# Scores of the third chunk computed early in fp32 and parked in DRAM, and key blocks of nearly equal size, in a top-k attention followed by two MLPs

## The chip, the cores and the metric

The kernel runs on one core of one Trainium2 chip. The metric is the device time of one launch in microseconds (us); the median of three runs of the kernel before is 1254.39 us (1254.22 to 1255.24).

## What is computed

Four batches of eight heads, 576 positions, 64 numbers to a head. For every query row only the 32 largest of the 576 scores are kept, the softmax is taken over those, and the result of all heads goes, token by token, through two MLPs with 2304 tokens, a model width of 512 and a hidden width of 2048.

```python
scores = scale * np.matmul(q, k.transpose(0, 1, 3, 2))
kth = np.partition(scores, -top_k, axis=-1)[..., -top_k:-top_k + 1]
scores = np.where(scores >= kth, scores, -1000000000.0)
attn = np.exp(scores - np.max(scores, axis=-1, keepdims=True))
attn = attn / (np.sum(attn, axis=-1, keepdims=True) + 1e-09)
x = np.matmul(attn, v)            # to (B * S, H * D)
h = x @ w_in;  g = h - np.tanh(h);                                     x = g @ w_out
h = x @ w_in2; g = np.where(h > 0, h, np.exp(np.minimum(h, 0)) - 1);   out = g @ w_out2
```

## The kernel before

The 2304 tokens are cut into six chunks of 384 tokens (chunk 0 to chunk 5; "the third chunk" is chunk 2, all of batch 1, tokens 192 to 575). A chunk has four pairs of heads, and each pair has two groups of three query tiles (128 query rows by 576 scores each), so there are 48 groups, numbered `g.at` 0 to 47; groups 16 to 23 are chunk 2. In chunks 0, 2, 3 and 5 a unit (`Unit`) is one head of a pair, and so is a group; in chunks 1 and 4 a unit holds 192 rows of both heads.

For every tile `scores` (L286) makes the 128x576 scores in two halves of 288. Chunk 0 (`u.whole`) multiplies fp32 operands directly, one matmul call for a half (L297; the profile shows two rows for each fp32 call). All later chunks first split q and k into two fp32r parts (`split_qk` at L257: ScalarE copies, GpSimd subtracts; tiles `qs`, `kk`) and use two fp32r matmuls for a half (L299, L300). ScalarE copies each half from PSUM (tile `ps`) to the score tile `s` in SBUF (L301), of which there are seven.

The search (`topk_steps`, L303) runs on VectorE: four rounds, in each a MAX8 that finds the next eight maxima (L322), and after the first three a MATCH_REPLACE that takes them out (L336). Then the mask is applied: by VectorE (L343), or by ScalarE (L338, L339) for all tiles of most groups of chunk 0. `transposed` (L345) transposes the masked weights `e` in five blocks of keys with TensorE (L364) and copies them out as `ph` (L365); `attend` (L367) multiplies each block of keys of `ph` with the same block of v (`vraw`) (L386), both heads side by side in the columns of the array. The blocks are 128, 128, 128, 128 and 64 keys.

The MLPs follow a chunk behind: `first` (L458) is the first product of a step (twelve matmuls of 384 columns into `h`, L471), ScalarE evaluates the nonlinearity (`t`), `gate` (L480) combines both on VectorE (L485, L490), ScalarE and GpSimd split it into `gh` and `gl` (L130, L131), and `second` (L496) accumulates nine matmuls of 512 columns into `acc` (L507). Each chunk has 2 x 16 such steps; `between` (L513) turns the first MLP's output into the second's input (`zh`, `zl`). The weights are not stored as fp32r, so in the first stretch and during chunk 0's MLPs `prepare` (L154) unpacks them: load `wr`, ScalarE (L165, L166, L170), GpSimd (L168), VectorE (`wf`, L171), split (`wp`), and a store to a scratch in DRAM (L176), from where later chunks load them (`wt`, L187).

What stands where in the program is set by ticks: a group's search takes four ticks (round r of group n is tick 4n + r), and tables `before`, `mid`, `late`, `ends` name what else is issued at a tick. A list scheduler then orders the instructions of each engine by priority, which follows this order of issue; from there each engine takes its instructions in that fixed order. All DMAs of the program are issued by SyncE (SP), also in one fixed order, and a DMA whose wait isn't met holds up those behind it.

Of the kernel before, what the change touches and what calls it, by code (L numbers as in the profile page):

```python
# [8 lines left out]
F32 = mybir.dt.float32  # L9
# [88 lines left out]
def tile_topk_attention_two_mlps(  # L98
# [34 lines left out]
    def bank(tag, name, bufs):  # L133
        return ps.tile([P, 512], F32, tag=tag, name=name, bufs=bufs)
# [63 lines left out]
    for ci, size in enumerate(SIZES):  # L198
        for p in range(NPAIR):
            row = []  # L200
            c0 = 0
            for b, q0, n in CHUNKS[ci]:
                for heads in ([[0], [1]] if n >= 256 else [[0, 1]]):
                    u = Unit()
                    u.ci, u.b, u.p, u.q0, u.heads, u.c0, u.n = ci, b, p, q0, heads, c0, n
                    u.id = f"{ci}_{p}_{b}_{q0}_{heads[0]}"
                    u.whole = ci < WHOLE
                    u.last = False
                    u.k = n * len(heads) // P
                    row.append(u)  # L210
                c0 += n
# [27 lines left out]
    def quick(u):  # L239

        return u.ci < QUICK and u.p == NPAIR - 1 and u.g.at == chunk_end[u.ci] - 1

    def load_q(u):
        u.qraw = sb.tile([P, NU], F32, tag="qraw", name=f"qraw{u.id}", bufs=QR_BUFS)
        src = qT[u.b, 2 * u.p + u.heads[0] : 2 * u.p + u.heads[-1] + 1, :, u.q0 : u.q0 + u.n].rearrange("h d s -> d h s")
        nq = u.n * len(u.heads)
        for half in range(1 if u.whole else 2):
            nc.sync.dma_start(u.qraw[half * D : half * D + D, :nq].rearrange("d (h s) -> d h s", s=u.n), src)

    def load_k(u):  # L250
        u.kraw = {}
        for h in u.heads:
            u.kraw[h] = sb.tile([P, S], F32, tag="kraw", name=f"kraw{u.id}_{h}", bufs=KR_BUFS)
            for half in range(1 if u.whole else 2):
                nc.sync.dma_start(u.kraw[h][half * D : half * D + D], kT[u.b, 2 * u.p + h])

    def split_qk(u):  # L257

        if u.whole:
            return  # L260
        u.kh, u.kl = {}, {}
        nq = u.n * len(u.heads)
# [14 lines left out]
    def segments(u, t):  # L277
# [5 lines left out]
                out.append((lo, hi, h, t * P + lo - i * u.n))  # L283
        return out

    def scores(u, t):  # L286
        if t == 0:
            u.s = []
        s = sb.tile([P, S], F32, tag="s", name=f"s{u.id}_{t}", bufs=S_BUFS)
        u.s.append(s)  # L290
        for half in range(2):
            cs = slice(half * HS, half * HS + HS)
            for lo, hi, h, _ in segments(u, t):
                pt = bank("at", f"ps{u.id}_{t}_{half}_{h}", 3)
# [395 lines left out]
```

## Time and profile before

| | us |
|---|---|
| median of three runs | 1254.39 |
| the profiled execution | 1255.49 |
| its span, first to last instruction | 1253.7 |
| TensorE (PE) busy | 1173.3 |
| VectorE (DVE) busy | 981.0 |
| ScalarE (ACT) busy | 783.6 |
| GpSimd (POOL) busy | 605.1 |

The profiled execution took 1.8 us more than its span, and 1.1 us more than the median. TensorE's busy time counts overlapping matmuls once, and a busy TensorE may still be at half clock. The mean granted clock over the span is 0.969 of 2.4 GHz.

### The profile page before, as it was taken

What the parts mean: (1) busy time and instruction counts of PE and PEld (TensorE: products, weight loads), DVE (VectorE), ACT (ScalarE), POOL (GpSimd) and SP (SyncE); (2) the same over time, 40 slices, a digit from 0 to 9 for tenths busy, and PEclk for the clock granted to TensorE, in tenths of its full rate; (3) what the DMA queues carried; (4) which work ended last, traced back from release to release, by engine and by line L of the source; (5) the groups of instructions that cost most, each with busy time, mean ns of one, the idle gap of its engine ahead of it and who ended that gap; (6) DMA issues with size and microseconds to landing.
All of it is one profiled execution on the core that took longest, in us unless ns stands there. A gap on an engine that the chain in (4) does not pass through costs nothing.

```text
span 1253.7 us, 19743 instructions
## 1 busy us (share of the span) xinstructions
PE 1173.3 (94%) x6424; PEld 982.7 (78%) x6424; DVE 981.0 (78%) x1951; ACT 783.6 (63%) x1716; POOL 605.1 (48%) x629
## 2 busy tenths in 40 slices
PE   4477889999999999999999999999999999999998
PEld 2243468877879888988888989888888888889897
DVE  7899999999999999959989768899779998100111
ACT  5898878789776557545566565666555565332333
POOL 4787459978994433333433344434334422223222
PEclk9975689998999999999999999999999999999999
DMA  7987247986779775667656778667667545687672
GB/s 238 319 285 251 84 155 233 354 274 222 265 245 358 238 227 168 226 223 262 213 195 204 236 229 271 217 190 239 210 225 259 198 153 179 208 273 254 219 248 79
DMA packets 97446, 286.12 MB, mean 228 GB/s; under 512 B 12096, under 2 KB 27968, under 8 KB 97344
## 3 DMA queue, kind: packets, MB, share of 16 engines
q1 hardware_dynamic: 97344, 284.87, 68.5%
q8 instruction: 51, 0.84, 0.3%
q14 instruction: 51, 0.42, 0.1%
HBM read 246.55 MB, written 38.27 MB: 227 GB/s over the span
## 4 chain that ended last, share of the span: by engine, by line
PE 70%; ACT 8%; DVE 8%; DMA 6%; POOL 5%; issue 3%; SPq 0%; ACTq 0%; POOLq 0%; DVEq 0%
PE acc L507 28%; PE h L471 28%; PE av L386 6%; DMA wr<-in_w_dram 5%; PE pt L364 4%; DVE vm L322 3%; DVE w L336 2%; PE ps L299 2%; PE ps L300 2%; POOL wr L168 2%; DVE wf L171 1%; ACT s L301 1%; ACT wr L166 1%; POOL kk L131 1%; ACT ph L365 1%
## 5 line engine op out<-in xcount | busy, mean ns | idle before, releaser
L131 POOL TENSOR_TENSOR gl<-g,gh 128x384 fp32r<-128x384 f32 x192 | 205.1, 1070 | 356.8 <-ACT gh L130 322.4
L322 DVE MAX8 vm<-w 128x8 f32<-128x576 f32 x432 | 317.9, 750 | 3.3
L507 PE MATMUL acc<-wt,gh 128*128 128x512 f32 x1008 | 269.0, 397 | 0.4 <-ACT gh L130 0.3
L336 DVE MATCH_REPLACE8 w<-vm,w 128x576 f32<-128x576 f32 x288 | 213.0, 740 | 0.0
L507 PEld LDWEIGHTS acc<-wt,gh 128*128 128x128 f32 x1008 | 184.7, 188 | 34.6 <-issue 3.9
L364 PE MATMUL pt<-ident,e 128*128 128x128 f32 (+1 forms) x720 | 120.1, 297 | 46.7 <-ACT e L339 35.5
L130 ACT ACTIVATE gh<-g 128x384 fp32r<-128x384 f32 x192 | 100.5, 524 | 80.0 <-DVE g L485 45.4
L301 ACT ACTIVATE s<-ps 128x288 f32<-128x288 f32 (+1 forms) x320 | 122.1, 407 | 43.6 <-PE ps L300 36.1
L485 DVE SCALAR_TENSOR_TENSOR g<-t,h 128x384 f32<-128x384 f32 x96 | 52.0, 543 | 123.8 <-ACT t L477 123.8
L507 PE MATMUL acc<-wt,gl 128*128 128x512 f32 x504 | 148.8, 398 | 0.0
L471 PE MATMUL h<-zh,wt 128*128 128x384 f32 (+2 forms) x768 | 146.7, 325 | 1.6 <-ACT zh L526 0.9
L364 PEld LDWEIGHTS pt<-ident,e 128*128 128x128 f32 (+1 forms) x720 | 89.8, 145 | 71.5 <-ACT e L339 42.2
L322 DVE MAX8 vm<-s 128x8 f32<-128x576 f32 x144 | 108.0, 750 | 47.1 <-ACT s L301 46.6
L471 PE MATMUL h<-xh,wt 128*128 128x384 f32 x672 | 141.9, 338 | 0.0
L471 PEld LDWEIGHTS h<-zh,wt 128*128 128x128 f32 x768 | 124.9, 189 | 9.1 <-ACT zh L526 2.4
L365 ACT ACTIVATE ph<-pt 128x384 f32<-128x384 f32 (+1 forms) x240 | 109.6, 491 | 25.3 <-PE pt L364 24.3
L471 PEld LDWEIGHTS h<-xh,wt 128*128 128x128 f32 x672 | 117.9, 188 | 7.1 <-issue 0.6
L343 DVE SCALAR_TENSOR_TENSOR e<-s,vm,e 128x576 f32<-128x576 f32 x115 | 116.3, 1017 | 1.6 <-ACT e L326 0.8
L476 ACT ACTIVATE t<-h 128x384 f32<-128x384 f32 x96 | 46.5, 486 | 102.6 <-PE h L471 102.5
L507 PEld LDWEIGHTS acc<-wt,gl 128*128 128x128 f32 x504 | 92.6, 188 | 18.3 <-issue 0.6
L336 DVE MATCH_REPLACE8 w<-vm,s 128x576 f32<-128x576 f32 x144 | 106.7, 741 | 0.0
L168 POOL TENSOR_TENSOR wr<-wr,tiny 128x512 f16<-128x512 f32 x64 | 90.1, 1410 | 31.8 <-ACT wr L166 28.5
(80 smaller groups left out, 2019.3 us busy)
## 6 DMA issues: line engine op xcount, KB each, us to landing
wt<-w SPq DMA_DIRECT2D x336, 512.0 KB, 4.3
wr<-in_w_dram SPq DMA_DIRECT2D x64, 512.0 KB, 5.3
w<-wp SPq DMA_DIRECT2D x64, 512.0 KB, 4.3
kraw<-in_kT_dram SPq DMA_DIRECT2D x120, 144.0 KB, 4.2
vraw<-in_vL_dram SPq DMA_DIRECT2D x64, 160.0 KB, 3.0
qraw<-in_qT_dram SPq DMA_DIRECT2D x88, 96.0 KB, 3.4
out_dram<-o SPq DMA_DIRECT2D x16, 256.0 KB, 5.4
out_dram<-o SPq DMA_DIRECT2D x4, 128.0 KB, 4.9
```

Of the source, the lines that this page charges most:

```text
L130: nc.scalar.activation(hi, src, copy)
L131: nc.gpsimd.tensor_sub(lo, src, f(hi))
L168: nc.gpsimd.tensor_mul(top, scaled, tiny)
L301: nc.scalar.activation(s[lo:hi, cs], pt[lo:hi, :HS], copy)
L322: nc.vector.max(g.vm[:, j, min(r, 1)], u.s[t] if r == 0 else g.w[j])
L336: nc.vector.match_replace(g.w[j], v, u.s[t] if r == 0 else g.w[j], FILL)
L343: nc.vector.scalar_tensor_tensor(u.e[t], u.s[t], v[:, 7:8], u.e[t], op0=ALU.is_ge, op1=ALU.mult, accum_out=g.sum[:, j : j + 1])
L364: nc.tensor.transpose(pt[:kn, j * P : j * P + P], v.e[t][:, k0 : k0 + kn], ident)
L365: nc.scalar.activation(g.ph[:kn, blk, :nq], pt[:kn, :nq], copy)
L386: nc.tensor.matmul(banks[c0][h * D : h * D + D, : v.n], v.vraw[h][:kn, blk], v.g.ph[:kn, blk, cs], start=(blk == order[0]), stop=(blk == o ...
L471: nc.tensor.matmul(h[:, cs], wv[:, wi, kt], xs[:, kt, cs], start=(a == 0), stop=(a == len(jobs) - 1))
L507: nc.tensor.matmul(acc[ci, m][t], gx[:, t * P : t * P + P], wt[:, wi], start=(ft == 0 and k == 0), stop=(ft == NF - 1 and k == 2),)
```

## The change

Two things change. First, the blocks of keys become 116, 116, 116, 116 and 112 (the host lays out v for them; a block is still stored and loaded with 128 rows). Second, the scores of groups 16 to 23 (`PARK`) are no longer made just ahead of their search. They are made while chunk 0 is searched, from tick 4 on, a unit every 3.5 ticks, at a priority lowered by 300 places (`later`): `park` multiplies in fp32 as chunk 0 does, into PSUM banks of the tag `h`, ScalarE copies the halves to a tile `sp` (two buffers), and SP stores that to DRAM (`sd`). Where `scores` made the tile before, it now loads it: one DMA from `sd` to `s`. These units load q and k once instead of twice, to tiles of their own with one buffer each (tags `qp`, `kp`), and are not split.

```diff
-KBLK = [(0, 128), (128, 128), (256, 128), (384, 128), (512, 64)]
+KBLK = [(0, 116), (116, 116), (232, 116), (348, 116), (464, 112)]
...
+PARK = range(16, 24)
+PARK_AT = 4
+PARK_STEP = 3.5
+PARK_BUFS = 2
+PARK_LOW = 300
...
     def load_q(u):
-        u.qraw = sb.tile([P, NU], F32, tag="qraw", name=f"qraw{u.id}", bufs=QR_BUFS)
+        u.qraw = sb.tile([P, NU], F32, tag="qp" if parked(u) else "qraw", name=f"qraw{u.id}", bufs=1 if parked(u) else QR_BUFS)
...
-        for half in range(1 if u.whole else 2):
+        for half in range(1 if u.whole or parked(u) else 2):
...
     def split_qk(u):
 
-        if u.whole:
+        if u.whole or parked(u):
             return
...
+    def park(u, t):
+
+        s = sb.tile([P, S], F32, tag="sp", name=f"sp{u.id}_{t}", bufs=PARK_BUFS)
+        products(u, t, s, True)
+        u.parked[t] = dr.tile([P, S], F32, tag=f"sd{u.id}_{t}", name=f"sd{u.id}_{t}")
+        nc.sync.dma_start(u.parked[t], s)
+
     def scores(u, t):
         if t == 0:
             u.s = []
         s = sb.tile([P, S], F32, tag="s", name=f"s{u.id}_{t}", bufs=S_BUFS)
         u.s.append(s)
+        if parked(u):
+            nc.sync.dma_start(s, u.parked[t])
+        else:
+            products(u, t, s, u.whole)
+
+    def products(u, t, s, whole):
+
         for half in range(2):
...
-                pt = bank("at", f"ps{u.id}_{t}_{half}_{h}", 3)
+                pt = bank("h", f"pp{u.id}_{t}_{half}_{h}", 2) if parked(u) else bank("at", f"ps{u.id}_{t}_{half}_{h}", 3)
...
+            if parked(u):
+                at = PARK_AT + PARK_STEP * parks[0]
+                parks[0] += 1
+                on(before, int(at) - 3, lambda u=u: (load_q(u), load_k(u)))
+                for t in range(u.k):
+                    on(ends, int(at + t * PARK_STEP / 3), lambda u=u, t=t: later(park, u, t))
+            else:
+                on(before, max(-6, t0 - lead) if u.whole else t0 - lead, lambda u=u: (load_q(u), load_k(u)))
+                on(before, t0 - 5, lambda u=u: split_qk(u))
```

The change moves instructions beyond the lines of the diff, since the scheduler orders each engine anew. Three places follow.

ScalarE, in the first stretch, where the weights of the first steps are unpacked (`sc`, `wr`, `wp`) beside chunk 0's scores (`s`). Before:

```order
L301 ACTIVATE s_1_0_0_0_0_246<-ps_1_0_0_0_0_0_0_247 128x288
L165 ACTIVATE sc_14_0_543<-wr_14_0_540 128x512
L166 ACTIVATE wr_14_0_540<-wr_14_0_540 128x512
L301 ACTIVATE s_1_0_0_0_0_246<-ps_1_0_0_0_0_1_0_250 128x288
L130 ACTIVATE wp_13_0_443<-wf_13_0_437 128x512
L130 ACTIVATE wp_13_1_455<-wf_13_1_449 128x512
L165 ACTIVATE sc_14_1_555<-wr_14_1_552 128x512
L166 ACTIVATE wr_14_1_552<-wr_14_1_552 128x512
```

The same place now:

```order
L330 ACTIVATE s_1_0_0_0_0_254<-ps_1_0_0_0_0_0_0_255 128x288
L175 ACTIVATE sc_14_1_643<-wr_14_1_640 128x512
L176 ACTIVATE wr_14_1_640<-wr_14_1_640 128x512
L330 ACTIVATE s_1_0_0_0_0_254<-ps_1_0_0_0_0_1_0_258 128x288
L140 ACTIVATE wp_14_0_636<-wf_14_0_630 128x512
L330 ACTIVATE sp_0_1_192_1_0_365<-pp_0_1_192_1_0_0_1_366 128x288
L330 ACTIVATE sp_0_1_192_1_0_365<-pp_0_1_192_1_0_1_1_369 128x288
L330 ACTIVATE sp_0_1_192_1_1_438<-pp_0_1_192_1_1_0_1_439 128x288
```

The copies to `sp` of parked tiles stand between those of the weights; all 48 of them come before the first copy of chunk 1's scores, 6 of them before the first copy of group 2's.

SP, a little later in the same stretch: loads of weights (`wr`) and stores of unpacked ones (`w`). Before:

```order
L156 DMA wr_15_0_623<-in_w_dram 128x512
L156 DMA wr_15_1_635<-in_w_dram 128x512
L176 DMA w_13_1_100<-wp_13_1_455 128x1024
L176 DMA w_14_0_101<-wp_14_0_548 128x1024
L156 DMA wr_0_0_713<-in_w_dram 128x512
```

And now:

```order
L166 DMA wr_15_0_742<-in_w_dram 128x512
L186 DMA w_13_1_100<-wp_13_1_525 128x1024
L166 DMA wr_15_1_754<-in_w_dram 128x512
L306 DMA sd_0_1_192_1_0_372<-sp_0_1_192_1_0_365 128x576
L186 DMA w_14_0_101<-wp_14_0_636 128x1024
L166 DMA wr_0_0_845<-in_w_dram 128x512
```

Stores of parked tiles (`sd`) now stand between the loads of weights.

VectorE, in chunk 0's second MLP, between the gates of its steps 11 and 12 (`g0_1_11`, `g0_1_12`; names with their numbers; `vm2_...` and `w32_...` belong to chunk 2's search). Before:

```order
L485 SCALAR_TENSOR_TENSOR g0_1_11_3776<-t0_1_11_3760,h0_1_11_3747 128x384
L322 MAX vm2_0_2_0_1_192_0_3870<-w32_0_2_0_1_192_0_1_3874 128x8
L336 MATCH_REPLACE w32_0_2_0_1_192_0_1_3874<-vm2_0_2_0_1_192_0_3870,w32_0_2_0_1_192_0_1_3874 128x576
L322 MAX vm2_0_2_0_1_192_0_3870<-s2_0_1_192_0_2_3767 128x8
L322 MAX vm2_0_2_0_1_192_0_3870<-w32_0_2_0_1_192_0_1_3874 128x8
L336 MATCH_REPLACE w32_0_2_0_1_192_0_2_3875<-vm2_0_2_0_1_192_0_3870,s2_0_1_192_0_2_3767 128x576
L171 SCALAR_TENSOR_TENSOR wf1_13_1_3525<-wr1_13_1_3523 128x512
L322 MAX vm2_0_2_0_1_192_0_3870<-w32_0_2_0_1_192_0_2_3875 128x8
L171 SCALAR_TENSOR_TENSOR wf1_14_0_3638<-wr1_14_0_3636 128x512
L336 MATCH_REPLACE w32_0_2_0_1_192_0_2_3875<-vm2_0_2_0_1_192_0_3870,w32_0_2_0_1_192_0_2_3875 128x576
L485 SCALAR_TENSOR_TENSOR g0_1_12_3843<-t0_1_12_3832,h0_1_12_3819 128x384
```

And now, the twelve rows that end with the same gate:

```order
L181 SCALAR_TENSOR_TENSOR wf1_13_0_3750<-wr1_13_0_3748 128x512
L351 MAX vm2_0_2_0_1_192_1_4329<-w32_0_2_0_1_192_1_0_4332 128x8
L351 MAX vm2_0_2_0_1_192_0_4067<-w32_0_2_0_1_192_0_2_4072 128x8
L351 MAX vm2_0_2_0_1_192_0_4067<-w32_0_2_0_1_192_0_1_4071 128x8
L365 MATCH_REPLACE w32_0_2_0_1_192_1_0_4332<-vm2_0_2_0_1_192_1_4329,w32_0_2_0_1_192_1_0_4332 128x576
L365 MATCH_REPLACE w32_0_2_0_1_192_0_2_4072<-vm2_0_2_0_1_192_0_4067,w32_0_2_0_1_192_0_2_4072 128x576
L372 SCALAR_TENSOR_TENSOR e2_0_1_192_0_1_4118,sum2_0_2_0_1_192_0_4069<-s2_0_1_192_0_1_3906,vm2_0_2_0_1_192_0_4067,e2_0_1_192_0_1_4118 128x576
L365 MATCH_REPLACE w32_0_2_0_1_192_1_1_4333<-vm2_0_2_0_1_192_1_4329,s2_0_1_192_1_1_4143 128x576
L181 SCALAR_TENSOR_TENSOR wf1_13_1_3761<-wr1_13_1_3759 128x512
L351 MAX vm2_0_2_0_1_192_1_4329<-w32_0_2_0_1_192_1_0_4332 128x8
L351 MAX vm2_0_2_0_1_192_0_4067<-w32_0_2_0_1_192_0_2_4072 128x8
L514 SCALAR_TENSOR_TENSOR g0_1_12_4046<-t0_1_12_4035,h0_1_12_4022 128x384
```

The search of chunk 2 is further on at the same gate: group 17 (`vm2_..._1`) is under way beside group 16. Counted over the whole order, 13 more instructions of the search (MAX8, MATCH_REPLACE, mask) stand ahead of this gate than before, 15 more ahead of the gate of step 15, 12 more ahead of `zl1` (the subtraction in `between` of chunk 1), 0 to 5 more ahead of the gates of steps 5 to 9 of its second MLP, and from chunk 2's second MLP on the order on VectorE is that of before.

## Rows read from the trace of the kernel before

**Rows 1.** The page: engines' busy us; a group's busy us, mean ns, idle before.

```profile
PE 1173.3 (94%) x6424; PEld 982.7 (78%) x6424; DVE 981.0 (78%) x1951; ACT 783.6 (63%) x1716; POOL 605.1 (48%) x629
...
L322 DVE MAX8 vm<-w 128x8 f32<-128x576 f32 x432 | 317.9, 750 | 3.3
```

**Rows 2.** Stretches: length, busy us per engine, granted clock, DMA share, GB/s.

```profile
22.00:150.00 128.00, 80.64 (x232) 41.54 (x233) 120.24 (x244) 107.20 (x231) 87.15 (x97) 0.76 0.75 249
...
178.00:300.00 122.00, 117.22 (x691) 101.60 (x690) 120.11 (x231) 100.53 (x216) 104.09 (x102) 0.96 0.81 271
300.00:378.00 78.00, 73.15 (x430) 60.27 (x429) 74.19 (x130) 63.51 (x136) 72.01 (x61) 0.98 0.76 256
378.00:473.00 95.00, 94.90 (x540) 82.25 (x538) 91.31 (x191) 56.59 (x130) 37.21 (x41) 1.00 0.80 270
473.00:558.00 85.00, 83.70 (x477) 72.00 (x477) 69.73 (x143) 49.60 (x111) 30.46 (x34) 1.00 0.61 201
558.00:1106.00 548.00, 545.72 (x3184) 473.46 (x3183) 448.04 (x908) 321.30 (x719) 209.05 (x225) 1.00 0.67 218
```

**Rows 3.** Waits of VectorE, 0 to 150 us: total, times, longest.

```profile
DVE vm L322 <- ACT s L301: 12.0, 9, 5.7
```

**Rows 4.** Groups by line and form, 331 to 484 us: busy us, mean ns, idle before.

```profile
L301 ACT ACTIVATE s<-ps 128x288 f32<-128x288 f32 x47 | 17.6, 410 | 6.8 <-PE ps L300 6.5
...
L299 PE MATMUL ps<-kk,qs 128*128 128x288 f32 x48 | 14.8, 317 | 0.7 <-ACT ph L365 0.7
...
L131 POOL TENSOR_TENSOR kk<-kraw,kk 128x576 fp32r<-128x576 f32 x7 | 10.0, 1428 | 0.4
...
L265 POOL TENSOR_TENSOR qs<-qraw,qs 64x384 fp32r<-64x384 f32 x7 | 7.4, 1061 | 23.9 <-ACT qs L264 22.6 <-DVE g L485 1.3
```

**Rows 5.** TensorE in order of time around 391 us: start, duration, instruction.

```profile
390.87 0.29 PE L299 MATMUL ps<-kk,qs 128*128 128x288 f32 x1
...
391.14 0.34 PE L471 MATMUL h<-xh,wt 128*128 128x384 f32 x1
```

**Rows 6.** TensorE instructions of L299 in one stretch.

```profile
473.00:484.00 11.00, 2.11 (x6) 1.12 (x6) 1.00 0.44 142
```

**Rows 7.** TensorE in order of time around 668 us, from two stretches.

```profile
667.07 3.60 PE L386 MATMUL av<-ph,vraw 64*64 64x384 f32 x20
...
667.86 2.80 PE L386 MATMUL av<-ph,vraw 128*64 128x384 f32 x16
...
670.59 0.96 PE L507 MATMUL acc<-wt,gh 128*128 128x512 f32 x3
```

**Rows 8.** Groups by line and form, 473 to 1253.7 us: blocks of 64 keys.

```profile
L386 PE MATMUL av<-ph,vraw 64*64 64x384 f32 x40 | 8.6, 508 | 0.0
...
L386 PE MATMUL av<-ph,vraw 64*64 64x192 f32 x32 | 6.0, 345 | 0.0
```

**Rows 9.** Groups by line on TensorE, 22 to 150 us.

```profile
L297 PE MATMUL ps<-kraw,qraw 64*128 64x288 f32 x68 | 36.4, 687 | 7.7 <-ACT ph L365 5.3 <-ACT s L301 2.3
```

**Rows 10.** Waits of ScalarE, 22 to 150 us.

```profile
ACT sc L165 <- DMA wr<-in_w_dram: 9.4, 7, 3.6
ACT wr L166 <- DMA wr<-in_w_dram: 4.3, 4, 2.4
```

**Rows 11.** DMA, 22 to 150 us.

```profile
DMA packets 11016, 31.89 MB, mean 249 GB/s; under 512 B 1345, under 2 KB 3393, under 8 KB 11008
```

**Rows 12.** Masking by VectorE (groups by line): 300 to 378, then 378 to 473 us.

```profile
L343 DVE SCALAR_TENSOR_TENSOR e<-s,vm,e 128x576 f32<-128x576 f32 x7 | 10.7, 1541 | 0.0
...
L343 DVE SCALAR_TENSOR_TENSOR e<-s,vm,e 128x576 f32<-128x576 f32 x15 | 13.1, 881 | 0.1
```

**Rows 13.** Waits of SP's queue, 300 to 378 us.

```profile
SPq L176 <- POOL wp L131: 28.9, 15, 5.8
```

**Rows 14.** Waits of TensorE, 473 us to the end.

```profile
PE ps L299 <- ACT ph L365: 1.5, 3, 0.7
```

**Rows 15.** The chain that ended last, in order of time: start, us, what.

```profile
158.43 2.35 PE h L471 x12
```

More of the change, by code (lines that the diff above doesn't have):

```diff
@@ L207, in tile_topk_attention_two_mlps @@
                     u.whole = ci < WHOLE
+                    u.parked = {}
                     u.last = False
@@ L241, in quick, with parked @@
         return u.ci < QUICK and u.p == NPAIR - 1 and u.g.at == chunk_end[u.ci] - 1
+    def parked(u):
+        return u.g.at in PARK
     def load_q(u):
-        u.qraw = sb.tile([P, NU], F32, tag="qraw", name=f"qraw{u.id}", bufs=QR_BUFS)
+        u.qraw = sb.tile([P, NU], F32, tag="qp" if parked(u) else "qraw", name=f"qraw{u.id}", bufs=1 if parked(u) else QR_BUFS)
         src = qT[u.b, 2 * u.p + u.heads[0] : 2 * u.p + u.heads[-1] + 1, :, u.q0 : u.q0 + u.n].rearrange("h d s -> d h s")
         nq = u.n * len(u.heads)
-        for half in range(1 if u.whole else 2):
+        for half in range(1 if u.whole or parked(u) else 2):
             nc.sync.dma_start(u.qraw[half * D : half * D + D, :nq].rearrange("d (h s) -> d h s", s=u.n), src)
@@ L252, in load_k @@
         for h in u.heads:
-            u.kraw[h] = sb.tile([P, S], F32, tag="kraw", name=f"kraw{u.id}_{h}", bufs=KR_BUFS)
-            for half in range(1 if u.whole else 2):
+            u.kraw[h] = sb.tile([P, S], F32, tag="kp" if parked(u) else "kraw", name=f"kraw{u.id}_{h}", bufs=1 if parked(u) else KR_BUFS)
+            for half in range(1 if u.whole or parked(u) else 2):
                 nc.sync.dma_start(u.kraw[h][half * D : half * D + D], kT[u.b, 2 * u.p + h])
     def split_qk(u):
-        if u.whole:
+        if u.whole or parked(u):
             return
@@ L293, in scores @@
             for lo, hi, h, _ in segments(u, t):
-                pt = bank("at", f"ps{u.id}_{t}_{half}_{h}", 3)
+                pt = bank("h", f"pp{u.id}_{t}_{half}_{h}", 2) if parked(u) else bank("at", f"ps{u.id}_{t}_{half}_{h}", 3)
                 qc = slice(t * P, t * P + P)
-                if u.whole:
+                if whole:
                     nc.tensor.matmul(pt[:, :HS], u.qraw[0:D, qc], u.kraw[h][0:D, cs], start=True, stop=True)
@@ L576, in on, with later @@
         table.setdefault(tick, []).append(do)
+    parks = [0]
+    def later(do, *a):
+        with tc.high_priority(offset=-PARK_LOW):
+            do(*a)
     for g in groups:
@@ L581, in tile_topk_attention_two_mlps @@
             lead = 6 if u.whole else 8
-            on(before, max(-6, t0 - lead) if u.whole else t0 - lead, lambda u=u: (load_q(u), load_k(u)))
-            on(before, t0 - 5, lambda u=u: split_qk(u))
+            if parked(u):
[7 more added lines that the diff above has]
+                on(before, t0 - 5, lambda u=u: split_qk(u))
             on(before, t0 + (1 if hurried(u) else 3), lambda u=u: load_v(u))
```

## The prediction

> **What bounds the kernel now.** I read the page first, then the stretches, then the waits, then single lines. The page makes TensorE the busiest engine by far, at 94% of the span, with VectorE at 78% [rows 1]; those are averages over stretches that differ. The stretches show it [rows 2]. In the first stretch, while chunk 0 is searched, VectorE sets the pace: 120.2 of 128 us up to 150 us. What it waits for there is a score tile from ScalarE, 12.0 us in nine waits up to 150 us, the longest of 5.7 at the very start [rows 3]. From 178 to 473 us, chunk 0's MLPs and the first MLP of chunk 1, two engines are nearly full at once: VectorE stands idle for 122 - 120.1, 78 - 74.2 and 95 - 91.3 us, 9.4 of 295, and TensorE for 9.7. From 473 us on TensorE alone is full (83.7 of 85, 545.7 of 548) and VectorE has room [rows 2]. So a microsecond saved on TensorE is worth a microsecond after 473 us; between 178 and 473 us only if VectorE, which does the same work as before, can come earlier too; and before that nothing, while a microsecond lost there by VectorE is lost for good.
>
> **What is removed on TensorE.** Chunk 2 has 24 tiles of two halves, 48 pairs of fp32r matmuls, all between 331 and 484 us [rows 4]. Where a pair stands between two matmuls of an MLP, the first starts at 390.87 and the next other matmul at 391.14 [rows 5]: 0.27 us a pair. Six pairs lie after 473 us [rows 6], 6 x 0.27 = 1.6 us; the other 42, 11.3 us, lie in the stretch where VectorE is full too. Taken away with them are two copies of q and k on ScalarE and the subtractions on GpSimd, 10.0 + 7.4 us for the seven units in the window [rows 4].
>
> **The key blocks.** A product of weights and v is twenty rows for five blocks. At 667.07 us the block of 64 keys goes first, and takes until 667.86: 0.79 us. The four blocks of 128 take until 670.59, 2.73 us or 0.68 each [rows 7]. With five blocks of one kind I expect five times 0.68, 0.11 less. The blocks of 64 after 473 us are 40 / 4 + 32 / 4 = 18 products [rows 8], so 18 x 0.11 = 2.0 us; bounds 0 and 0.15 for each (0.15 if the first of the four also lost something to the switch), 0 to 2.7. The row says that a block of 64 rows costs more than one of 128. The Trainium skill, TensorE: Matmul & The Clock Gate, section LDWEIGHTS (loading the stationary operand), has loads timed by columns, not by rows of contraction; by that alone equal blocks would be worth nothing and the sum would be 2.0 us less good. The number of blocks, transposes and copies stays five.
>
> **What is added in the first stretch.** 48 fp32 products on TensorE. Those of chunk 0 are 68 rows, 34 products, in 36.4 us: 1.07 each [rows 9], so up to 51 us, at a granted clock whose mean there is 0.76. TensorE has 47 us idle in that stretch [rows 2], so this fits only if the clock rises as TensorE becomes busier; nobody waits for it at once, and I price it at 0 with an upper bound of 4. 48 copies on ScalarE at 0.41 [rows 4], 19.7 us. Six of them stand ahead of group 2's scores, about where this stretch begins, and 42, 17.2 us, after that, ahead of chunk 1's. ScalarE is idle for 128 - 107.2 = 20.8 us there [rows 2], so 3.6 would be left. But 13.7 of the 20.8 are waits for weight loads [rows 10], and the queue becomes fuller: to 31.9 MB in that stretch [rows 11] come 24 stores of 0.295 MB and q and k for eight units, 2 MB, together 9.1, which takes the DMA share from 0.75 to 0.96. Behind a store that waits for its `sp`, the `wr` loads wait, and behind a waiting `sc` or `wr` on ScalarE the next `s` copy, for which VectorE waits. If all these waits were filled the head would end as before; if all 13.7 us of them stayed, it would end 13.7 - 3.6 = 10.1 us later. I take it that somewhat less than half stay, 6.1 us, since the copies stand between the loads' users in ScalarE's order: 6.1 - 3.6 = **+2.5 us**, bounds 0 and 10.1.
>
> **From 178 to 473 us.** TensorE could be 42 x 0.27 plus ten products x 0.11, 12.4 us, earlier. VectorE can't: in the new order twelve more search instructions stand ahead of `zl1`, which chunk 1's second MLP waits for, at 317.9 / 432 = 0.74 us each [rows 1]: +8.9 us. Against that stand its 9.4 us of idle time, and less contention: its masks took 1541 ns in 300 to 378 us and 881 afterwards [rows 12], when GpSimd went from 72 of 78 us to 37 of 95 [rows 2]. Seven masks at 0.66 are 4.6 us. About half of chunk 2's 17.4 us on GpSimd lie in that stretch, a tenth of its 72.0, so I take 1.0, for masks and unpacking together (bounds 0 and 4.6). VectorE thus comes to `zl1` 8.9 - 9.4 - 1.0 = **1.5 us earlier**, if it never idles. If half its idle time stays, it comes 3.2 later. If the order were no limit, TensorE would give 12.4.
>
> **After 473 us.** The surplus on VectorE is used up by the middle of the second MLP (0 to 5 instructions), so TensorE sets the pace: 1.6 + 2.0, and 1.0 for waits on ScalarE that disappear with chunk 2's scores (of 1.5 in all to the end [rows 14] I take two thirds to be chunk 2's): **4.6 us earlier**, bounds 1.6 and 6.
>
> **The loads** of 24 tiles replace chunk 2's q and k loads; 0.295 MB takes what those took, and the search reaches a tile up to a group later. I price them at 0. In the bound above they cost: between 300 and 378 us SP waits for GpSimd's `wp` 15 times, 28.9 us in all, up to 5.8 us at once [rows 13], and a load behind such a store is late for a MAX8 that heads VectorE's order.
>
> **The sum.** +2.5 - 1.5 - 4.6 = -3.6 on the profiled 1255.5: 1251.9; the median of the runs stands 1.1 us lower, so **1250.8**.
>
> **Rivals.**
> - Full release: the scheduler's order isn't binding, the head is hidden. 0 - 12.4 - 4.6 = -17: 1237.4, and by halves up to 1246. For it: TensorE at 94%. Against it: VectorE's 98% from 178 to 300 us. Chance 0.20.
> - The head grows (ends slower): the waits for loads stay and `s` comes later for each group. +10.1 - 1.5 - 4.6 = +4.0, 1258.4; with TensorE's 4 us 1262. It decides from +8.6 us on, where the total passes +2.5. For it: DMA share 0.96, ScalarE's 3.6 us. Against it: the order puts copies where ScalarE waited. Chance 0.27.
> - VectorE gives the gain back: half its idle time stays, or the loads are late behind `wp`. 2.5 + 3.2 - 4.6 = +1.1: 1255.5. Chance 0.13.
> - Equal blocks are worth nothing: -1.6, 1252.8, no change that can be told. The row at 667 us speaks against it, one switch of the array's shape beside another could speak for it. The rule of the Trainium skill's page TensorE: Matmul & The Clock Gate, quoted above, would make it so. Chance 0.07.
> - The forecast: 0.33.
>
> A measurement of this kernel tells a change from none at about 0.2%, 2.5 us. Faster by more: the forecast and full release, 0.53. Within: 0.20. Slower: 0.27. The range, 1240 to 1262, leaves out the lowest of full release and the worst head.
>
> **What would show it.** In the profile after: chunk 0's first MLP matmul (at 158.4 us before [rows 15]) 2 to 3 us later, and ScalarE's idle time to 150 us near 6 us; more than 8 us later makes the head the story. The first `zl` of chunk 1 about 1 us later than before; if it comes 8 or more earlier, VectorE's order was not binding and the forecast is too high. Products of weights and v of 3.4 us in place of 3.52. From 560 us on the same distance to before to within 2 us. A rise of VectorE's waits for `s` between 300 and 473 us, now on DMA, would show the loads late. Wrong it would be most of all in the head, whose price rests on how many of ScalarE's waits can be filled.

## The result: 0.9907 of the time before

The changed kernel takes 1244.11 us (median of six, 1242.62 to 1247.1); the kernel before, beside it on the same chip, 1255.13 us (1254.22 to 1259.65). The ratio is 0.9907, 95% interval 0.9893 to 0.9921. The medians are 11.0 us apart, the profiled executions (1255.49 and 1243.85 us) 11.6. The forecast was 1250.8 in a range of 1240 to 1262, so the sign and the range hold, but the likeliest value is 7 us too high: the gain is three times the 3.6 us that were forecast.

The page of the changed kernel, engines' busy us, and its stretches, with the columns of [rows 2]:

```profile
PE 1191.5 (96%) x6424; PEld 999.4 (80%) x6424; DVE 975.6 (79%) x1951; ACT 773.8 (62%) x1700; POOL 583.8 (47%) x613
```

```profile
22.00:150.00 128.00, 109.28 (x291) 62.18 (x290) 116.42 (x227) 113.19 (x260) 84.45 (x94) 0.80 0.89 308
...
178.00:300.00 122.00, 114.54 (x697) 102.56 (x696) 122.00 (x235) 101.80 (x221) 105.47 (x103) 0.96 0.83 274
300.00:378.00 78.00, 69.99 (x423) 56.38 (x422) 77.08 (x142) 65.15 (x136) 70.24 (x64) 1.00 0.79 274
378.00:473.00 95.00, 94.14 (x506) 79.95 (x505) 95.00 (x204) 45.17 (x96) 28.22 (x35) 0.98 0.86 308
473.00:558.00 85.00, 84.87 (x483) 73.92 (x482) 69.36 (x148) 46.36 (x105) 27.71 (x30) 1.00 0.64 206
558.00:1106.00 548.00, 545.69 (x3209) 480.56 (x3208) 438.73 (x888) 321.27 (x718) 212.34 (x226) 1.00 0.71 221
```

Against [rows 2] the first stretch has lost VectorE 3.8 us (120.24 to 116.42) though ScalarE does more (107.20 to 113.19); from 178 to 473 us VectorE has 0.9 us of idle time left of 9.4.

Where the time went is read from the first matmul of each MLP half on TensorE, in order of time (start, duration, instruction); two of these rows, and `zl` on VectorE:

```profile
166.59 1.01 PE L500 MATMUL h<-xh,wp 128*128 128x384 f32 x2
...
472.67 1.10 PE L500 MATMUL h<-zh,wt 128*128 128x256 f32 x7 [0.82 <-ACT zh L555]
```

```profile
473.52 0.68 DVE L556 TENSOR_TENSOR zl<-yt,zh 128x512 fp32r<-128x512 f32 x1
```

Such starts, in us (m0 and m1 are the two MLPs of a chunk; the head is all that lies ahead of chunk 0's m0):

| start of | before | after | after minus before |
|---|---|---|---|
| chunk 0 m0 | 158.4 | 166.6 | +8.2 |
| chunk 0 m1 | 271.8 | 277.8 | +6.0 |
| chunk 1 m0 | 378.1 | 384.4 | +6.3 |
| chunk 1 m1 (its `zl` on VectorE) | 473.0 (472.5) | 472.7 (473.5) | -0.4 (+1.0) |
| chunk 2 m0 | 557.9 | 553.3 | -4.7 |
| chunk 3 m0 | 740.8 | 734.8 | -6.0 |
| chunk 4 m0 | 931.1 | 920.0 | -11.1 |
| chunk 5 m1 | 1179.4 | 1167.8 | -11.6 |

So there are three parts: a head that ends 8.2 us later, 8.6 us won back by 473 us, and 11.2 us won after it.

### The profile page after: what moved, and what is told of

Its sections match the earlier page's. It is cut to its first block, busy times and chain, and to the rows that moved or that the text cites. A ratio compares the mean times of both kernels' runs of the same rounds, so it can differ in the third digit from the quotient of the medians.

```text
span 1242.1 us, 19800 instructions
## 1 busy us (share of the span) xinstructions
PE 1191.5 (96%) x6424; PEld 999.4 (80%) x6424; DVE 975.6 (79%) x1951; ACT 773.8 (62%) x1700; POOL 583.8 (47%) x613
## 4 chain that ended last, share of the span: by engine, by line
PE 74%; DVE 8%; ACT 6%; DMA 6%; POOL 3%; issue 2%; SPq 1%; ACTq 0%; POOLq 0%; DVEq 0%
PE acc L536 28%; PE h L500 28%; PE av L415 5%; PE pt L393 5%; DMA wr<-in_w_dram 4%; DVE vm L351 3%; DVE w L365 2%; PE ps L328 2%; PE pp L326 2%; PE ps L329 2%; DMA kraw<-in_kT_dram 1%; DVE wf L181 1%; PE ps L326 1%; POOL wr L178 1%; ACT ph L394 1%
## 5 line engine op out<-in xcount | busy, mean ns | idle before, releaser
L393 PE MATMUL pt<-ident,e 128*116 128x128 f32 (+1 forms) x720 | 119.0, 293 | 18.5 <-ACT s L330 6.1
L330 ACT ACTIVATE s<-ps 128x288 f32<-128x288 f32 (+1 forms) x272 | 106.3, 412 | 41.1 <-PE ps L329 33.1
L394 ACT ACTIVATE ph<-pt 116x384 f32<-116x384 f32 (+1 forms) x240 | 110.6, 498 | 31.1 <-PE pt L393 30.0
L393 PEld LDWEIGHTS pt<-ident,e 128*116 128x116 f32 (+1 forms) x720 | 90.2, 143 | 45.6 <-ACT s L330 10.0
L372 DVE SCALAR_TENSOR_TENSOR e<-s,vm,e 128x576 f32<-128x576 f32 x115 | 113.3, 990 | 1.4 <-ACT e L355 0.6
```

What stands on the lines that cost most here:

```text
L372: nc.vector.scalar_tensor_tensor(u.e[t], u.s[t], v[:, 7:8], u.e[t], op0=ALU.is_ge, op1=ALU.mult, accum_out=g.sum[:, j : j + 1])
L393: nc.tensor.transpose(pt[:kn, j * P : j * P + P], v.e[t][:, k0 : k0 + kn], ident)
L394: nc.scalar.activation(g.ph[:kn, blk, :nq], pt[:kn, :nq], copy)
```

## The experiments

Twelve kernels, in three groups on one chip each; each ratio is to the kernel before on that chip. "Searches ahead" counts the search instructions that stand ahead of chunk 1's `zl` in VectorE's written order: 507 before, 519 after.

**e1_blocks** and **e2_park** take the two halves of the change apart. Both keep the order of their parent on every engine.

```diff
# e1_blocks: before
-KBLK = [(0, 128), (128, 128), (256, 128), (384, 128), (512, 64)]
+KBLK = [(0, 116), (116, 116), (232, 116), (348, 116), (464, 112)]
# e2_park: the changed kernel, with the old line
```

> The kernel before with the five nearly equal key blocks alone; every engine's order is that of before. Theory A (read from the two traces: a product of one piece became 0.14 us shorter, the two-piece products of chunk 4 1.0 to 1.3 us shorter, and TensorE is full from 473 us on): 14 x 0.14 + 4 x 1.15 = 6.6 us, so 1248.5 against 1255.1, all of it after 473 us. Rival B (the price of the prediction, 0.11 for each of 18 products): 2.0 us, 1253.1. Rival C (blocks worth nothing, what the two-piece products gained came from elsewhere): 1255.1.

Measured: 0.9956 (0.994 to 0.9973), 5.5 us. The trace of the kernel before has ten products of one piece after 473 us, not the fourteen of the expectation, so Theory A comes to 10 x 0.14 + 4 x 1.15 = 6.0 us.

> The changed kernel with the old key blocks (four of 128 and one of 64); every engine's order is that of the changed kernel. Theory A (the two halves of the change add up): 1244.1 + 6.6 = 1250.7 us, with chunk 0's first MLP matmul near 166.6 and the gain of 178 to 473 us kept at about 8. Rival B (blocks worth 2.0): 1246.1. Rival D (the blocks' shorter products also helped between 178 and 473 us, where chunk 1 has four two-piece products): 1252 to 1255, with less than 5 us won between 178 and 473 us.

Measured: 0.995 (0.9933 to 0.9968), 6.3 us. The halves add up: 0.9956 x 0.995 = 0.9906. Theory A holds in both, as far as the intervals tell. The changed kernel and e2_park differ in the trace by 0.2 us at chunk 3's m0 (734.8 and 735.0) and by 5.2 at chunk 4's m0 (920.0 and 925.2): the blocks pay almost wholly where chunk 4's products run. TensorE in order of time, a two-piece product (one whose 384 columns go in two pieces of 192) of chunk 4 in e2_park, then in the changed kernel, then one of one piece in the changed kernel:

```profile
873.12 4.54 PE L415 MATMUL av<-ph,vraw 64*64 64x192 f32 x40
```

```profile
869.85 0.38 PE L415 MATMUL av<-ph,vraw 112*64 112x192 f32 x1
869.96 0.27 PE L459 MATMUL rt<-ident,r 128*64 128x128 f32 x1
870.06 3.48 PE L415 MATMUL av<-ph,vraw 112*64 112x192 f32 x39
...
661.29 3.45 PE L415 MATMUL av<-ph,vraw 112*64 112x384 f32 x20
```

A one-piece product went from 3.60 [rows 7] to 3.45 us, the upper bound of the forecast. The two-piece ones, which [rows 7] do not show, went from 4.5 or 4.8 to 3.5 or 3.7 (here from 869.85 to 873.54), 0.85 to 1.3 us each, 4.5 for chunk 4's four. Inside the 4.54 us the starts of the single matmuls show why: one piece's blocks of 64 keys stand among the other's of 128, so the rows in use change three times (five times in the products of 4.8 us), and each time the next matmul starts 0.25 us after the last, where otherwise two matmuls, one for each head, start every 0.16 us; next to the changes they start singly, 0.16 to 0.21 us apart.

**e7_blocks96** asks whether it is the 64 rows or the inequality.

```diff
# before
+KBLK = [(0, 128), (128, 128), (256, 128), (384, 96), (480, 96)]
```

> The kernel before with key blocks of 128, 128, 128, 96 and 96. Theory A (the cost is that of a block of 64 rows between blocks of 128, and 96 rows are laid out like 128): as with five nearly equal blocks, ratio 0.9956, two-piece products of chunk 4 at 3.5 us in place of 4.8. Rival U (any change of the rows between blocks costs): two-piece products stay at 4.5 to 4.8 us, ratio 0.998 to 1.0.

Measured: 0.9957 (0.9942 to 0.9971), and a two-piece product of chunk 4 takes as long as with equal blocks:

```profile
878.13 0.38 PE L386 MATMUL av<-ph,vraw 96*64 96x192 f32 x1
878.23 0.27 PE L430 MATMUL rt<-ident,r 128*64 128x128 f32 x1
878.34 3.48 PE L386 MATMUL av<-ph,vraw 96*64 96x192 f32 x39
```

So the cost is that of the block of 64, not of unequal blocks: 96 and 128 rows side by side take no longer than 116 and 112.

**e3_free** leaves out the early work, and with it what makes the head late, but keeps chunk 2's scores out of their old place.

```diff
-            nc.sync.dma_start(s, u.parked[t])
+            nc.sync.dma_start(s, kT[u.b, 2 * u.p : 2 * u.p + 2].rearrange("h d s -> (h d) s"))
...
-                on(before, int(at) - 3, lambda u=u: (load_q(u), load_k(u)))
-                for t in range(u.k):
-                    on(ends, int(at + t * PARK_STEP / 3), lambda u=u, t=t: later(park, u, t))
```

> The changed kernel without the head's part: the early q and k loads, the 48 fp32 products, the 48 copies and the 24 stores are left out, and chunk 2's search loads 24 tiles of the same size from k in DRAM instead, so its values are not those of the reference. The scheduler puts some instructions of the first stretch in another order with it. Theory A (the head's cost of 8.2 us is carried through to the end, since VectorE is full from 178 to 473 us): 1244.1 - 8.2 = 1235.9 us, chunk 0's first MLP matmul back at 158.4. Rival E (the lateness is made up anyway between 178 and 473 us, where VectorE had 9.4 us of idle time before): 1240 to 1244, the first matmul at 158.4, and the stretch 178 to 473 us giving 4 to 8 us less than in the changed kernel.

Measured: 0.9912 (0.9893 to 0.9932), no faster than the changed kernel, though its head ends at 160.1 instead of 166.6. Theory A falls. What differs on the way is VectorE: 533 searches stand ahead of `zl` in its order, 14 more than in the changed kernel, and from 300 us on it is as good as full:

```profile
300.00:378.00 78.00, 70.39 (x424) 57.30 (x422) 76.82 (x140) 64.88 (x135) 69.30 (x60) 1.00 0.82 279
378.00:473.00 95.00, 91.65 (x500) 76.66 (x501) 95.00 (x209) 43.53 (x95) 28.70 (x34) 1.00 0.82 293
```

`zl` starts at 478.54, 5.0 us after the changed kernel's, and from chunk 1's m1 to chunk 3's m0 it takes 259.5 us in place of 262.1, since work done too early is not done later. In this order the head's 6.5 us are thus worth nothing at the end: what the early start gains is used up by VectorE's searches. A kernel with the changed kernel's order on VectorE and no early work was not run, so what the head costs with the order held fixed stays open.

**e4_nostore** was to tell stores from copies in the head.

```diff
 def park(u, t):
     products(u, t, s, True)
-    u.parked[t] = dr.tile([P, S], F32, tag=f"sd{u.id}_{t}", name=f"sd{u.id}_{t}")
-    nc.sync.dma_start(u.parked[t], s)
...
-            nc.sync.dma_start(s, u.parked[t])
+            nc.sync.dma_start(s, kT[u.b, 2 * u.p : 2 * u.p + 2].rearrange("h d s -> (h d) s"))
```

> The changed kernel with the early products and copies but without the 24 stores; chunk 2's search loads tiles of the same size from k in DRAM, so its values are not those of the reference. The scheduler puts some instructions of the first stretch in another order. Theory F (the head's cost is the DMA queue: stores of 7.1 MB ahead of the weight loads): nearly all 8.2 us come back, 1236 to 1238, first MLP matmul at 158 to 160. Theory G (it is ScalarE's 19.7 us of copies and the products ahead of them): almost nothing comes back, 1242 to 1244, first MLP matmul at 165 to 167. A half each would give 1240.

Measured: 1.0036 (1.0021 to 1.005). It fits neither theory. The first stretch has another order, in which TensorE stands behind early products whose k has not landed; its waits, 22 to 178 us:

```profile
PE pp L324 <- DMA kraw<-in_kT_dram: 9.0, 3, 4.5
```

The changed kernel has 4.6 us of this wait. The run tells nothing of the stores' share; without them, but in another order, the head ends 9 us later still, at 175.7 us.

**e8_poolq** takes the stores off SP's queue.

```diff
-        nc.sync.dma_start(u.parked[t], s)
+        nc.gpsimd.dma_start(u.parked[t], s)
```

> The changed kernel with the 24 stores issued from GpSimd's queue in place of SP's, so that no weight load stands behind a store that waits for its sp; the scheduler orders the first stretch anew, 519 search instructions stay ahead of chunk 1's zl. Theory Q (the head's 8.2 us are weight loads and unpacking held up behind waiting stores): the first MLP matmul at 160 to 163 us and the end 3 to 6 us before the changed kernel's, ratio 0.986 to 0.988. Rival G (it is ScalarE's copies, the products and VectorE's waits for them): first MLP matmul at 165 to 168 us, ratio 0.990 to 0.992; a store that waits at the head of GpSimd's queue holds up its subtractions, which could make it worse, 0.995.

Measured: 0.9923 (0.9896 to 0.995), first MLP matmul at 168.9. Theory Q is not borne out. But GpSimd itself now waits for the stores' tiles, 7.4 us of its waits from 22 to 150 us, so the run does not show that stores waiting at SP cost nothing there:

```profile
POOL sd L306 <- ACT sp L330: 4.4, 4, 1.4
POOL sd L306 <- ACT s L330: 3.0, 2, 2.1
```

**e11_fakeload** has the changed kernel's order on the four compute engines, with loads that depend on no store.

```diff
-            nc.sync.dma_start(s, u.parked[t])
+            nc.sync.dma_start(s, kT[u.b, 2 * u.p : 2 * u.p + 2].rearrange("h d s -> (h d) s"))
```

> The changed kernel with all of its early work and its stores, but the 24 loads take tiles of the same size from k in DRAM, so that no load depends on a store, and chunk 2's values are not those of the reference. The orders of TensorE, VectorE, ScalarE and GpSimd are those of the changed kernel. Theory A (the loads are hidden): the changed kernel's ratio, 0.9907 within 0.0015. Rival L (a load late behind its store or in DRAM holds VectorE up): 1 to 3 us faster, 0.988 to 0.990.

Measured: 0.9888 (0.9869 to 0.9907); span 1241.8 against 1242.1, `zl` at 473.2 against 473.5. From chunk 1's m1 on all starts lie within 0.3 us of the changed kernel's, so the loads are hidden in the profiled execution; the interval alone would allow 2 us.

**e9_pairs** and **e10_split** give back one part each of what chunk 2's scores took; up to the middle of chunk 0's MLPs their order is that of the changed kernel.

```diff
# e9_pairs: behind the load of a parked tile, for each half and head
+                    pt = bank("at", f"ps{u.id}_{t}_{half}_{h}", 3)
+                    nc.tensor.matmul(pt[:, :HS], flat[:, :P], flat[:, P : P + HS], start=True, stop=False)
+                    nc.tensor.matmul(pt[:, :HS], flat[:, :P], flat[:, P : P + HS], start=False, stop=True)
# e10_split: for each unit of chunk 2 (True: the loads of before, in two halves)
+                on(before, t0 - 8, lambda u=u: (load_q(u, True), load_k(u, True)))
+                on(before, t0 - 5, lambda u=u: split_qk(u))
```

> The changed kernel with 48 pairs of fp32r products put back on TensorE where chunk 2's scores stood, on constant data, into the same PSUM banks, and read by nobody: no copies and no splits of q and k come back. The first stretch has the order of the changed kernel; behind it 532 search instructions of VectorE stand ahead of chunk 1's zl, 13 more than in the changed kernel. Theory T (the gain behind the head is TensorE's freed time): 48 x 0.27 = 13 us come back, ratio 1.000 to 1.002. Theory V (VectorE's order up to 473 us is the limit, and TensorE's time counts only after it): 13 x 0.68 = 8.8 us more at the zl, a quarter of it returned, and 1.6 for the six last pairs, ratio 0.995 to 0.998. Rival R (the gain is what ScalarE and GpSimd no longer do): 0.991 to 0.993.

Measured: 0.9953 (0.9938 to 0.9968), 8.1 us over e11_fakeload (1252.09 and 1244.02, same chip). The size is Theory V's; Theory T's 13 us lie outside the two intervals. `zl` starts at 485.82. VectorE is full up to there, and part of its surplus comes back later: from chunk 1's m1 to chunk 3's m0 it takes 258.3 us in place of 262.1. TensorE is as good as full there too, so the size alone tells the theories apart:

```profile
378.00:473.00 95.00, 94.90 (x532) 82.31 (x531) 95.00 (x203) 41.95 (x88) 30.38 (x36) 1.00 0.87 301
473.00:558.00 85.00, 83.26 (x492) 71.83 (x492) 77.11 (x162) 51.00 (x115) 26.36 (x29) 1.00 0.61 189
```

> The changed kernel with chunk 2's loads of q and k in two halves and their splits on ScalarE and GpSimd put back where they stood; nobody reads them. The products stay out. The first stretch has the order of the changed kernel; 543 search instructions stand ahead of chunk 1's zl, 24 more. Rival R (the relief of ScalarE and GpSimd is what the gain behind the head comes from): TensorE's waits on ScalarE and VectorE's waits return between 178 and 473 us without any change in VectorE's order mattering, ratio 0.995 to 0.998. Theory V (VectorE's order): 24 x 0.68 = 16 us more at the zl, a quarter returned, ratio 0.999 to 1.002. Theory T (TensorE's time alone): no change, 0.990 to 0.992.

Measured: 1.0043 (1.0027 to 1.0059), 19.9 us over e11_fakeload; beyond Theory V, which came nearest. The chunk's whole split, with no scores to wait for, moved into one stretch, chunk 0's m1, which took 126.1 us in place of 107.6. So did searches: VectorE has 129 of them in this stretch, 106 in e11_fakeload. The stretch in e10_split, then in e11_fakeload:

```profile
276.20:402.30 126.10, 106.06 (x599) 85.38 (x598) 123.46 (x232) 101.49 (x214) 114.81 (x104) 0.93 0.82 268
```

```profile
276.10:383.70 107.60, 97.38 (x569) 82.79 (x568) 106.67 (x196) 87.52 (x184) 93.22 (x86) 0.94 0.80 268
```

VectorE is full in both, and 16.8 of the 18.5 us are its busy time. GpSimd's groups there (busy us, mean ns, idle before), in e10_split from 276 to 402 us and in e11_fakeload from 276 to 384 us:

```profile
L141 POOL TENSOR_TENSOR kk<-kraw,kk 128x576 fp32r<-128x576 f32 x12 | 18.0, 1506 | 0.5 <-ACT kk L140 0.4
...
L282 POOL TENSOR_TENSOR qs<-qraw,qs 64x384 fp32r<-64x384 f32 x10 | 11.1, 1111 | 0.8
```

```profile
L141 POOL TENSOR_TENSOR kk<-kraw,kk 128x576 fp32r<-128x576 f32 x4 | 6.2, 1560 | 0.4 <-ACT kk L140 0.3
...
L280 POOL TENSOR_TENSOR qs<-qraw,qs 64x384 fp32r<-64x384 f32 x2 | 2.0, 1010 | 0.2
```

GpSimd has 20.9 us more of splits and is as good as full too, 87.5 of 90 us from 296 to 386 us. Either engine's added work is about the 18.5 us, and the run does not tell which of the two set the length. In the kernel before only 1 k and 2 q splits more stand in that stretch than after the change, so this is no measure of what the change won there.

**e5_late** and **e6_early** park half of the chunk.

```diff
-PARK = range(16, 24)
+PARK = range(20, 24)   # e5_late;  range(16, 20) in e6_early
```

> The changed kernel with only the last four of chunk 2's eight groups computed early (range(20, 24)); the first four have their scores in place as before. In this order 510 search instructions of VectorE stand ahead of chunk 1's zl, against 519 in the changed kernel and 507 before. Theory O (VectorE's order ahead of that zl is the limit up to 473 us, and the pairs after 473 us are worth what TensorE spends on them): the nine fewer instructions, 6.7 us, make up for the 24 pairs that are back, the head grows by 4 instead of 8, zl at 468 to 473 us, and the end is that of the changed kernel or up to 4 us earlier: ratio to before 0.988 to 0.991. Rival P (the gain goes by the number of tiles moved): half of the parking's 6.2 and all of the blocks' 5.5, ratio 0.993.

Measured: 1.0026 (1.001 to 1.0042).

> The changed kernel with only the first four of chunk 2's eight groups computed early (range(16, 20)); the last four, whose products lie from about 405 us on and past 473, are in place as before. 508 search instructions stand ahead of chunk 1's zl. Theory O: zl at 468 to 473 us as in the other half, but the six pairs after 473 us and the waits on ScalarE there stay, 2.6 us: ratio 0.991 to 0.994, about 2.6 us later at the end than with the last four. Rival P (by the number of tiles): 0.993, the same as with the last four.

Measured: 1.0001 (0.9988 to 1.0014). Both theories fail in both: half of the parking is 5.7 to 8.8 us worse than the blocks alone (0.9956). From chunk 1's m0 to its m1 the half pays its half (91.8 and 92.2 us; 94.6 in e7_blocks96 on the same chip, 88.3 in the changed kernel). But the heads end at 164.2 and 161.7 us (158.7 in e7_blocks96), and from there to chunk 1's m0 it takes 226.1 and 224.7 us, where e7_blocks96 takes 222.6 and the changed kernel 217.8. From the head's end to `zl` both take 317 us, as e7_blocks96 does (316.8), where the changed kernel, with more searches ahead of `zl`, takes 306.9. VectorE has idle time on the way, as before the change; its rows from 378 to 473 us in e5_late, then in e6_early:

```profile
378.00:473.00 95.00, 95.00 (x536) 80.87 (x533) 90.84 (x190) 49.85 (x110) 40.12 (x44) 1.00 0.91 303
...
378.00:473.00 95.00, 92.59 (x500) 78.88 (x499) 87.64 (x183) 47.50 (x105) 36.92 (x39) 1.00 0.81 273
```

So half of the parking won nothing ahead of `zl`, and what the head lost stayed lost. The written order of the first stretch differs from the changed kernel's in both, and what in the orders causes this is not settled.

**e12_mask321** tries to relieve VectorE.

```diff
-MASK_ACT = [3, 1, 0, 0, 0, 0]
+MASK_ACT = [3, 2, 1, 0, 0, 0]
```

> The changed kernel with one more mask of each group of chunk 1, and one of each of chunk 2, done by ScalarE in place of VectorE (two for one, eight and eight of them); 516 search instructions of VectorE stand ahead of chunk 1's zl, 3 fewer. Theory V (VectorE is the limit between 178 and 473 us, where it had 0.9 us of idle time): 2 to 6 us faster than the changed kernel, 0.986 to 0.989, the fastest so far. Rival S (ScalarE's two longer instructions for each mask, 0.76 us each, come ahead of the copies that TensorE and VectorE wait for): 2 to 8 us slower than the changed kernel, 0.992 to 0.997.

Measured: 0.9916 (0.9901 to 0.9932), 4.2 us over e11_fakeload. Slower, as Rival S has it. In chunk 0's m0, 115.8 us in place of 110.8, TensorE waits behind the longer work on ScalarE:

```profile
PE ps L328 <- ACT s L330: 5.4, 4, 3.3
PE acc L536 <- POOL gl L141: 2.4, 3, 1.9
```

Chunk 1's m0 is 5.5 us longer too (94.2 in place of 88.7), and VectorE, which was to be relieved, is idle for 9.9 us between the head and `zl`, in place of 0.9.

No version beat the changed kernel by more than the intervals allow.

## Why the prediction was right, step by step

The sign and the range came true, but not by three right terms. The errors of the first two, +5.7 and -5.7 us, cancel, which is luck; the third, after 473 us, is off by -6.6 and makes most of the miss of 8.0 (the other 1.4 lie between `zl` and TensorE's first matmul of chunk 1's m1). The measured time lies inside what the rival of a full release was given (1237.4 to 1246), yet that rival's mechanism did not come: the head was not hidden, and `zl` came 1.0 us later than before and not 8 us earlier.

**The head, +2.5: mis-sized, +8.2** (+6.3 to +8.9 in the six kernels whose order there is the same or nearly). The step that failed is that ScalarE's idle time could all be filled but for waits on loads. ScalarE's waits, 22 to 150 us, in the changed kernel:

```profile
ACT sc L175 <- DMA wr<-in_w_dram: 5.5, 5, 1.9
ACT sp L330 <- PE pp L326: 2.2, 4, 0.9
ACT wr L176 <- DMA wr<-in_w_dram: 2.0, 1, 2.0
```

Of the 13.7 us on loads [rows 10] 7.5 stayed, where 6.1 were forecast, and the copies took what was forecast (43 of them, 16.7 us). But the other 7.1 us of idle time, 20.8 - 13.7, stayed as well: ScalarE is idle for 128 - 113.2 = 14.8 us, not near 6, of it 2.2 in new waits for the early products. The bound of 10.1 us, for all load waits staying, was thus nearly reached with half of them. The 48 products did fit on TensorE (109.3 of 128 us busy at a clock of 0.80); DMA share 0.89, not 0.96.

The path to VectorE was another one too. The forecast had VectorE wait longer for `s`. VectorE's waits from 0 to 150 us, one of before that stands beside [rows 3], then two of the changed kernel:

```profile
DVE wf L171 <- POOL wr L168: 2.6, 3, 1.8
```

```profile
DVE vm L351 <- ACT s L330: 11.2, 6, 5.7
DVE wf L181 <- POOL wr L178: 5.4, 4, 2.0
```

The waits for `s` did not grow (12.0 before); those for weights that GpSimd unpacks did. Up to chunk 0's m0 VectorE is idle for 19.4 us in place of 15.6, 3.8 of the 8.2 us. The other 4.4 are busy time for nearly the same work (178 searches in place of 177): a MAX8 or MATCH_REPLACE takes 0.69 us from start to start in place of 0.67, and 34 instructions in place of 4 start only after the end of the one ahead. Why fewer lay ready is not shown.

**178 to 473 us, -1.5: mis-sized; `zl` of chunk 1 +1.0, as forecast.** Behind the longer head VectorE came to `zl` 7.2 us sooner, where 1.5 was forecast (TensorE's first matmul of m1 8.6 sooner). Of VectorE's idle time 8.5 of 9.4 us went, much as the forecast's value had it. Not foreseen was that an instruction costs less than its duration when its neighbour is ready. VectorE in order of time, before, then after:

```profile
468.64 0.74 DVE L336 MATCH_REPLACE8 w<-vm,w 128x576 f32<-128x576 f32 x1
469.42 0.76 DVE L322 MAX8 vm<-w 128x8 f32<-128x576 f32 x1
470.21 0.09 DVE L336 MATCH_VALUE_LOAD w<-vm,w 128x8 f32 x1
470.29 0.74 DVE L336 MATCH_REPLACE8 w<-vm,w 128x576 f32<-128x576 f32 x1
```

```profile
467.38 0.73 DVE L365 MATCH_REPLACE8 w<-vm,w 128x576 f32<-128x576 f32 x1
468.04 0.74 DVE L351 MAX8 vm<-w 128x8 f32<-128x576 f32 x1
468.70 2.06 DVE L351 MAX8 vm<-s 128x8 f32<-128x576 f32 x3
```

Before, the MAX8 here needs the result of the MATCH_REPLACE ahead and the load needs the MAX8's; each starts 0.03 to 0.04 us after the end it waits for, 0.78 us after that one's start. After, with tiles that lie ready, the neighbours belong to other tiles and start 0.66 to 0.69 us apart. Between the head and `zl` 39 of 296 MAX8 and MATCH_REPLACE had such a successor before, none of 306 after. In sum over that way: idle time -8.5; durations +5.5, for eleven more searches and somewhat shorter unpacking, where 8.9 - 1.0 was forecast; overlap of neighbours -4.1, where nothing was forecast. The forecast took every instruction at its duration, the added ones and those already there; the failed step is this one. TensorE's 30 pairs of chunk 1's m0 are 8.1 us by the forecast's price, and that stretch went from 94.9 to 88.3 us; what of it is theirs is not shown, since VectorE is full there.

That VectorE's order ahead of `zl` decides is borne out in part. All kernels, from the first MLP matmul to `zl` (tied: MAX8 and MATCH_REPLACE whose successor starts only after their end):

| kernel | us to `zl` | searches on the way | VectorE idle, us | tied |
|---|---|---|---|---|
| before | 314.1 | 330 | 9.4 | 39 |
| e1_blocks | 319.3 | 330 | 13.9 | 36 |
| e7_blocks96 | 316.8 | 331 | 15.6 | 34 |
| e5_late | 317.4 | 333 | 10.3 | 17 |
| e6_early | 316.7 | 331 | 12.2 | 19 |
| changed | 306.9 | 341 | 0.9 | 0 |
| e2_park | 306.9 | 341 | 0.6 | 0 |
| e11_fakeload | 307.9 | 341 | 0.9 | 0 |
| e8_poolq | 312.1 | 343 | 1.5 | 1 |
| e4_nostore | 318.0 | 342 | 5.5 | 1 |
| e9_pairs | 318.5 | 354 | 1.0 | 1 |
| e3_free | 318.4 | 356 | 3.6 | 3 |
| e10_split | 327.9 | 365 | 3.9 | 0 |
| e12_mask321 | 313.0 | 338 | 9.9 | 29 |

Where VectorE is full, more searches ahead make `zl` later: e9_pairs, e3_free and e10_split have 13, 15 and 24 more than the changed kernel and come 11.6, 11.5 and 21.0 us later, most of it what these searches cost at 0.67 each. But the count alone does not decide. The five kernels at the top have eight to eleven fewer than the changed kernel and come 7 to 12 us later, with VectorE idle for 9 to 16 us and 17 to 39 of its searches tied; e4_nostore has one more and comes 11 us later. So what the change won ahead of `zl` is that VectorE ran there without a pause on tiles that lay ready. The kernels that load all 24 tiles of chunk 2 largely share this (at most 5.5 us idle and 3 tied), but for e12_mask321; those that load half or none don't. Neither the pairs nor the splits put back undo it (e9_pairs, e10_split); ScalarE's copies of chunk 2's scores were not put back alone, so whether their absence is what does it stays open. The three kernels with the order of before differ by 5 us, which is how far a single execution can be trusted here.

**After 473 us, -4.6: mis-sized, -11.2** from chunk 1's m1 on. The blocks: 2.0 forecast, 5.5 (e1_blocks) measured. The step that failed took every product for one of one piece, and counted the 32 rows of 192 columns [rows 8] as eight products; they are four of two pieces. For the ten of one piece 0.15 each, 1.5, is near the forecast, and chunk 4's four gave 4.5, together 6.0. The rest: 2.6 forecast, 4.9 in e2_park. Counted from start to start up to chunk 3's m0, the six pairs are 2.1 of it (1.6 forecast), waits of TensorE 1.1 (1.0), and 2.0, not foreseen, are fifteen transposes, a group's, that TensorE has behind it by 473 us now (150 rows of `pt` from there to chunk 3's m0, 165 before); the matmuls of `h` take 0.7 back. The forecast's sign, that from 560 us on the distance to before stays within 2 us, failed: it grew from 4.7 to 11.6.

**The loads, 0: right** (e11_fakeload). VectorE waits for no parked tile from 178 to 473 us.

**The rivals.** Full release, -17, did not come, and the pairs put back in e9_pairs cost 8.1 us, not 13. The head did grow, to within 0.4 of the point named for a slower kernel, 8.6, but was won back before `zl`. VectorE giving the gain back by idling did not happen here; in e5_late and e6_early half of the parking shows it. Equal blocks worth nothing is refuted by e1_blocks and e7_blocks96: the rule of the Trainium skill, TensorE: Matmul & The Clock Gate, section LDWEIGHTS (loading the stationary operand), that the columns and not the rows set the load's time, says nothing of the change from 64 rows to 128, which is what costs here.

## What to carry to other kernels

Where two in-order engines are full together, look at three things up to the place where both meet: how many instructions stand ahead of it in each order, how long each engine idles on the way, and how often an instruction waits for the one just ahead. Price instructions from start to start in the stretch that counts, not by their durations. Look for the slowest form of a group before pricing it; four products of 40 matmuls were worth more here than ten of 20. A lateness ahead of such a stretch can be won back in it, and an early start can be lost in it, so neither is carried to the end unseen.

## What the hardware showed that was not expected

Changing the rows in use from 64 to 128 and back costs TensorE some 0.1 us each time between matmuls of 192 columns (0.25 us from start to start in place of 0.16 for two). With the matmuls that start singly beside it, a product with three changes loses 0.85 to 1.0 us, and one with five 1.3; 128 and 96 rows side by side, and 116 and 112, show no such cost.

VectorE starts a search instruction that does not need the last one's result 0.07 to 0.09 us before that one's end, and one that does 0.03 to 0.04 us after it: 0.67 against 0.78 us for the same MAX8. The Trainium skill, VectorE: DVE Perf Modes, section The DRAIN you can't avoid, reports no gain from leaving out the semaphores between chained operations, and says that "A next op that is not held starts earlier". The trace fits the second: interleaving tiles was worth 0.1 us for each instruction that would else have waited for the last result.
